# Per-partition scales for the two output weights, y's quarter sums with one operand from PSUM, and the order planned anew

## The chip, the cores and the metric

The kernel runs on 1 core of a Trainium2 chip. The metric is the device time of one execution in microseconds, the median of 3 runs. Engines: PE (matrix products), PEld (its weight loads), DVE (vector), ACT (activation), POOL (general), SP (transfers).

## The reference, cut to what matters

```python
scores = scale * q @ k.transpose(0, 1, 3, 2)          # 4 batches, 8 heads, 576 x 64
scores = where(scores >= max(scores) - tau, scores, -1e9)
x = softmax(scores) @ v                               # to 2304 tokens x 512
h = x @ w_in                                          # 512 x 2048
x = (h * tanh(log1p(exp(min(h, 20))))) @ w_out        # layer 1; h itself over 20
h = x @ w2_in
out = (h * clip(h + 3, 0, 6) / 6) @ w2_out            # layer 2
```

The four weights arrive as 64-bit floats; everything else is 32-bit.

## The kernel before, in words

**Number format.** A product of 32-bit numbers is made as three products of 16-bit halves: each operand is scaled by a power of two and split into a high and a low half (`hi` on ACT, `lo`, a subtraction, on POOL or DVE). The scales need maxima.

**Weights.** The matrices are numbered m = 0 (w_in), 1 (w_out), 2 (w2_in) and 3 (w2_out), and come in 8 groups each of 128 partitions x 1024 pairs of words (`raw_lr`). `maximum` (L442, DVE) finds the largest value of each partition. `group_scale` makes a scale from it: a cut to the exponent (`cut`, L453), then `spread`, then `factor` (L456 to L460). `spread` gives every partition the maximum over all 128: `diag` puts the column on a diagonal matrix (tasks `zd`, tile `dgb_zd`, on ACT L413 or DVE L415), `total` multiplies it by ones on PE (`zp`, L418) and `top` takes the row maximum on DVE (`zt`, L421). Steps `c1` to `c4` then join the two words of each number. `summary` combines the eight groups' scales of a matrix. For m = 2 and 3, `combined` makes sums of quarters of the weights (tiles `sum_h`, `sum_q`).

**Stages.** Attention runs from 0 to about 430 us with the first matmul of layer 1 (`h_g`, L834) laid between its score tiles (`s_s`, L1448) and products with v (`aux_pv`, L1496); the exponentials pass to the latter through transposing DMAs (`pt_tr`). Layer 1's second matmul (`y_y`, L948) runs from 486 to 702 in 9 blocks of 256 tokens, 192 matmuls each, with two y tiles in PSUM. Weights of m = 1, 2 and 3 are converted under both. Layer 2 runs from 713: 7 products of quarters instead of 8 for each unit (`h_g0a`, `hp_g1a` and so on, L1021, 24 matmuls each; then L1168), whose operands are sums of quarters.

**y to layer 2.** `split_sums` takes the maximum of a block of y (L664), spreads it (`zpy`, the same PE step), copies the scaled block from PSUM to `xf` on ACT (`take`, L728), forms four quarter sums (`four_sums`, L703 and L383) and splits them (`yl_zhy`). The same `four_sums` makes the sums of the activated values (`g_ab`) in layer 2, on POOL.

**Order.** Every task goes to a planner (`Plan`) while the program is built. It holds a cost for each task and engine, due times and the constants at the head of the file, picks the engine where several may do a task (`WHO`), and so fixes the sequence of every engine. On the chip each engine runs its sequence in that order and stops at an instruction that is not ready. For the kinds of DVE tasks listed in `PORT` the planner reckons with no start ahead of the end of POOL's last task, which holds for the sums of `g_ab` and of the weights (`q`), and not for those of y:

```python
if e == "dve" and task.kind in PORT:
    t = max(t, self.clock["pool"])
```

Of the kernel before, what the change touches and what calls it, by code (L numbers as in the profile page):

```python
# [16 lines left out]
ALU = mybir.AluOpType  # L17
# [19 lines left out]
Q = BLK // 2  # L37
# [3 lines left out]
ORDER_OUT = (0, 5, 6, 4, 2, 3, 1)  # L41
INF_BITS = 0x7F800000
TINY = 2.0 ** -100
WARM_WINDOW = 3.413
RELEASE = dict.fromkeys(("s", "m", "h", "y", "aux"), 0.27)

STEP = 2.55
START = 7.2
PV_OFF = 3.72
V_FIRST = 1.0  # L50
DIRECT_AHEAD = 8.0
DIRECT = 1
PREP_AHEAD = 2.45
CONV_STEP = 2.06
CONV_AT = 3.0
LATE_STEP = 1.5
OUT_STEP = 2.39
OUT_AT = 0.0
V_AHEAD = 6.29
MOE_OFF = 9.75  # L60
MOE_LAG = 15.8
RATE = 1.32
NX = 3
FLIP = 1.61
ALPHA = {"act": 3.07, "pe": 6.71}
FITS = 0.09
# [19 lines left out]
SLACK = 0.26
SLOW = 0.75
SLOW_LATE = 0.162
HASTE = -9.076
WHO = {  # L90
    "c20": ("pool", "dve"), "c21": ("pool",), "c30": ("dve",), "c31": ("pool", "dve"),
    "q2": ("dve",), "q3": ("pool", "dve"), "u20": ("pool", "dve"), "u21": ("pool",),
    "u30": ("pool",), "u31": ("pool", "dve"), "qy": ("dve",), "uy0": ("pool", "dve"), "uy1": ("pool", "dve"),
    "q": ("pool",), "o0": ("dve",), "o1": ("pool",),
}
NBLK_EARLY = 2 * B - 1
EASE = {"mk": -1.41, "ph": -0.76, "pl": -3.92, "tr": -1.06, "ex": 0.6, "s": -3.68, "th": -3.16}
P_LO = ("pool",)
EXPAND = {"act": 1.15}
BUFS = {"e": 3, "p16": 3}  # L100
LATE = {"gs": 2, "hl": 2, "h": 2, "y": 2}
WINDOW = {"pe": 0.26, "dve": 0.05, "act": 0.02, "pool": 0.15, "sp": 0.21}
NEAR_LATE = {"pe": 0.577, "dve": 0.049, "act": 0, "pool": 0.004, "sp": 0.21}
OFF_LATE = 0
OFF_FINAL = 22.457
LATE_AT = 2.5
OFF_SECOND = 27.972
# [71 lines left out]
class Plan:  # L179
# [157 lines left out]
def fused_kernel(ctx: ExitStack, tc, q, k, v, tau, w1i, w1o, w2i, w2o, out):  # L337
    nc = tc.nc
# [46 lines left out]
    def pick(which, **cost):  # L385
        return {e: cost[e] for e in WHO[which]}
# [5 lines left out]
    NG = NF // 2  # L392
# [11 lines left out]
    def bits(t):  # L404
        return t.bitcast(U32)
# [60 lines left out]
    def summary(task, m, after):  # L466

        w = wsc[m]  # L470
# [20 lines left out]
        return task({"dve": 1.6}, scales, after, [], f"zs{m}")  # L491
# [13 lines left out]
    def convert(m, src, pool, prio, off, ring):  # L505
        if m not in wsc:
            scale_columns(m)
        if m < 2:
            r_w[m] = Ring(f"w{m}_", maker(pool, f"w{m}_", [P, 2, 2, DM], F16), NG)
            wt[m] = [Buf(r_w[m]) for _ in range(NG)]  # L510
            for w in wt[m]:
                w.left += 1
        elif m == 2:
            r_w[m] = Ring(f"w{m}_", maker(pool, f"w{m}_", [P, 7, 2 * P], F16), 2 * NG)
        if m > 1:
            wt[m] = [(Buf(r_w[m]), Buf(r_w[m])) for _ in range(NG)]
# [72 lines left out]
    def combined(m, g, t, after, task):  # L589
# [103 lines left out]
    def four_sums(task, name, tile_of, bufs, after, width, who):  # L693


        def at(k):
            return tile_of()[:, :, k]

        def differ(e):
            sub(e, at(6), at(0), at(1))  # L700

        def add_right(e, dst, k):
            engine[e].tensor_tensor(at(dst), at(k), at(2), ALU.add)  # L703

# [12 lines left out]
    def split_sums(task, name, src, dst, inverse, ring, deps):
# [255 lines left out]
    def second_layer(blk):  # L973
# [117 lines left out]
        def finish(g, part, first, done):  # L1091
# [745 lines left out]
```

## Time and profile before

| | |
|---|---|
| median of 3 runs | 1054.19 us (1052.78 to 1055.12) |
| profiled execution | 1054.73 us; its span 1052.9 us, so 1.8 us lie around the span |
| busy, share of the span | PE 969.1 us (92%), DVE 782.6 (74%), ACT 667.7 (63%), POOL 638.1 (61%) |
| mean granted clock of PE | 0.965 of full speed |

The rows below are from that execution. A wait names the engine that released it last; the clock is the share of 2.4 GHz that was granted.

### The profile page before, as it was taken

How to read it: one execution, taken by the hardware profiler on the slowest of the kernel's cores; microseconds unless marked ns; L12 is line 12 of the kernel's file. 1: busy time of each engine (PE TensorE's matmuls, PEld its weight loads, DVE VectorE, ACT ScalarE, POOL GpSimd, SP SyncE). 2: the span in 40 equal slices, each digit the busy share in tenths (PEclk: the TensorE clock that was granted, in tenths of full speed). 3: DMA queues.
4: the chain of work that ended last, by engine and by line, in shares of the span. 5: the costliest groups of instructions: out<-in, count | busy, mean ns of one | idle time of the engine just before them, and what ended most of it. 6: DMA issues, size and time to landing. Idle time of an engine off the chain costs nothing.

```text
span 1052.9 us, 26050 instructions
## 1 busy us (share of the span) xinstructions
PE 969.1 (92%) x10790; PEld 857.7 (81%) x10790; DVE 782.6 (74%) x1385; ACT 667.7 (63%) x1048; POOL 638.1 (61%) x544
## 2 busy tenths in 40 slices
PE   4789799999899988999998999989999999999997
PEld 2566478888888877888887888779999999999985
DVE  5887788788878778758999999996464645545563
ACT  5666668799788887657777877736444444444441
POOL 1676856566565667634554677745757566564664
PEclk9997669999999999999999999989999999999998
DMA  9865959999999999985475656564011101101001
GB/s 267 181 167 132 223 119 220 222 247 240 202 233 211 197 221 214 249 296 222 161 255 195 215 198 241 212 239 150 2 57 56 28 31 57 57 1 57 22 16 27
DMA packets 199336, 166.85 MB, mean 158 GB/s; under 512 B 174129, under 2 KB 174641, under 8 KB 192817
## 3 DMA queue, kind: packets, MB, share of 16 engines
q1 hardware_dynamic: 199216, 165.18, 59.0%
q8 instruction: 85, 1.39, 0.5%
q14 instruction: 35, 0.28, 0.1%
HBM read 86.64 MB, written 36.04 MB: 117 GB/s over the span
## 4 chain that ended last, share of the span: by engine, by line
PE 50%; DVE 25%; DMA 13%; ACT 5%; issue 4%; POOL 3%; SPq 1%; DVEq 0%; ACTq 0%; POOLq 0%
DMA pt_tr<-p_ph 8%; PE s_s L1448 6%; PE h_g L834 6%; PE h_g0a L1021 5%; PE hp_g1a L1021 4%; PE aux_pv L1496 3%; DVE gs_h L928 3%; DVE e_ex L1470 3%; PE y_y L948 2%; PE h_g0d L1021 2%; PE hp_g1d L1021 2%; DVE nm_pk L1457 2%; POOL p_ph L383 2%; DMA v_lv<-in_v 2%; DMA raw_lr<-in_moe_w_out 1%
## 5 line engine op out<-in xcount | busy, mean ns | idle before, releaser
L383 POOL TENSOR_TENSOR p_ph<-e_ex,p_ph 128x128 f16<-128x128 f32 (+3 forms) x160 | 190.9, 1215 | 108.2 <-ACT p_ph L1475 79.1
L1168 PEld LDWEIGHTS <-gs_h 128*128 128x128 f16 x1512 | 147.2, 98 | 19.2 <-issue 2.2
L1021 PEld LDWEIGHTS <-w__h 128*128 128x128 f16 x2016 | 157.9, 99 | 5.5 <-issue 4.7
L1457 DVE TENSOR_REDUCE nm_pk<-s_s 128x1 f32<-128x576 f32 x144 | 105.9, 751 | 36.2 <-PE s_s L1448 35.6
L1470 DVE SCALAR_TENSOR_TENSOR e_ex<-s_s,thr_th,e_ex 128x576 f32<-128x576 f32 x144 | 112.2, 811 | 18.1 <-ACT thr_th L1462 12.4
L703 POOL TENSOR_TENSOR g_ab<-g_ab 128x256 f32<-128x256 f32 x72 | 60.3, 848 | 106.2 <-DVE g_ab L1108 104.9
L1467 ACT ACTIVATE e_ex<-s_s,nm_pk 128x576 f32<-128x576 f32 x144 | 104.1, 732 | 24.7 <-DVE nm_pk L1457 17.8
L1496 PEld LDWEIGHTS <-pt_tr 128*128 128x128 f16 x2016 | 84.2, 105 | 30.5 <-DMA pt_tr<-p_ph 24.2
L1496 PE MATMUL aux_pv<-vh,pt_tr 128*128 128x65 f16 (+1 forms) x1296 | 91.1, 207 | 18.4 <-DMA pt_tr<-p_ph 18.0
L1475 ACT ACTIVATE p_ph<-e_ex 128x576 f16<-128x576 f32 x144 | 94.9, 680 | 18.5 <-DVE e_ex L1470 13.2
L383 DVE TENSOR_TENSOR gs_h<-g_ab,gs_h 128x896 f16<-128x896 f32 x36 | 52.3, 1456 | 68.8 <-ACT gs_h L1118 68.8
L1021 PEld LDWEIGHTS <-w__u 128*128 128x128 f16 x1008 | 99.3, 99 | 0.0
L1118 ACT ACTIVATE gs_h<-g_ab 128x1792 f16<-128x1792 f32 x36 | 59.2, 1689 | 61.2 <-POOL g_ab L383 61.2
L383 POOL TENSOR_TENSOR gs_h<-g_ab,gs_h 128x896 f16<-128x896 f32 x36 | 85.2, 2385 | 8.8 <-ACT gs_h L1118 8.8
L1108 DVE SCALAR_TENSOR_TENSOR g_ab<-g_ab,f 128x512 f32<-128x512 f32 x72 | 59.9, 878 | 9.9 <-ACT g_ab L1102 9.9
L1102 ACT ACTIVATE g_ab<-g_ab,aux,hscales 128x512 f32<-128x512 f32 x72 | 53.1, 803 | 16.9 <-DVE g_ab L1049 16.9
L383 POOL TENSOR_TENSOR g_ab<-g_ab 128x256 f32<-128x256 f32 x72 | 59.1, 832 | 1.3
L882 ACT ACTIVATE he_t<-h_g,hin 128x512 f32<-128x512 f32 x68 | 46.5, 684 | 18.2 <-PE h_g L834 14.6
L928 DVE SCALAR_TENSOR_TENSOR gs_h<-hp_e,fscales,gs_h 128x512 f16<-128x512 f32 x72 | 52.2, 739 | 2.2 <-ACT gs_h L922 1.9
L919 ACT ACTIVATE hp_e<-hl_l 128x512 f32<-128x512 f32 x72 | 42.2, 594 | 15.6 <-DVE gs_h L928 15.4
L1448 PE MATMUL s_s<-kda_kh,qsa_qp 128*128 128x288 f32 x160 | 49.2, 326 | 1.7 <-DVE den_dt L1571 0.7
L1448 PE MATMUL s_s<-kda_lk,qsa_qp 64*128 64x288 f32 x80 | 35.6, 604 | 15.3 <-DVE e_ex L1470 8.2
(690 smaller groups left out, 2955.3 us busy)
## 6 DMA issues: line engine op xcount, KB each, us to landing
hd<-he_t SPq DMA_DIRECT2D x36, 512.0 KB, 3.5
hl_l<-hd SPq DMA_DIRECT2D x18, 1024.0 KB, 6.1
raw_lr<-in_moe_w_in SPq DMA_DIRECT2D x16, 1024.0 KB, 5.6
raw_lr<-in_moe_w_out SPq DMA_DIRECT2D x16, 1024.0 KB, 6.3
yd<-yl_zhy SPq DMA_DIRECT2D x9, 896.0 KB, 5.0
rk_lk<-in_k SPq DMA_DIRECT2D x12, 576.0 KB, 4.7
rq_lq<-in_q SPq DMA_DIRECT2D x12, 576.0 KB, 5.6
v_lv<-in_v SPq DMA_DIRECT2D x16, 320.0 KB, 4.7
```

The lines of the kernel that those rows point to most:

```text
L383: engine[e].tensor_tensor(dst, a, b, ALU.subtract)
L703: engine[e].tensor_tensor(at(dst), at(k), at(2), ALU.add)
L834: mm(hv[:, j, :], wj[:, wl, c * P : (c + 1) * P], x.tile[:, c, xl, :], start=j == 0 and n == 0, stop=j == 1 and n == 11, skip_group_check= ...
L928: nc.vector.scalar_tensor_tensor(s.tile[:, k, 1], g.tile.rearrange("p (a n) -> p a n", a=2), fs[:, fp : fp + 1], s.tile[:, k, 0], ALU.mult ...
L1021: mm(dst.tile[:, i * Q : (i + 1) * Q], wt[2][fp][wl].tile[:, right - 1, c * P : (c + 1) * P], x[xl].tile[:, c, left - 1], start=first and ...
L1168: mm(region(p), part[:, gl, left - 1], wt[3][fp][wl].tile[:, right - 1], start=fp == n == 0 and spot(p)[1] == 0, stop=fp == NG - 1 and n == 2,
L1448: mm(s[j].tile[:, half, :HALF], lh, rh[:, half * HALF : (half + 1) * HALF], start=m == 0, stop=m == len(terms) - 1,)
L1457: nc.vector.tensor_reduce(neg.tile[:, j : j + 1], sv(j), AX.XY, ALU.max, negate=True)
L1467: nc.scalar.activation(ev(j), sv(j), AF.Exp, bias=neg.tile[:, j : j + 1])
L1470: nc.vector.scalar_tensor_tensor(ev(j), sv(j), thr.tile[:, j : j + 1], ev(j), ALU.is_ge, ALU.mult)
L1475: nc.scalar.activation(p16.tile[:, js, :S], e_.tile[:, js], AF.Copy)
L1496: mm(ov[:, dst, :d], pt.tile[:, j, ch, :], part.tile[:, src, vc, :], start=i == j == ch == 0 and part is vh, stop=j == w - 1 and ch == 8, ...
```

## The change

It has three parts. First, for m = 1 and 3 the cut and the spread of each group go: each partition has a scale of its own, from its own maximum (with a floor of 2^-13), and `summary` takes the maximum over the groups in each partition and spreads that once (`zps`), after which a new task `rows` makes the factors. That removes 16 tasks each of `za`, `zp` and `zt`, with their diagonals, and adds 2 `zps`. Second, the four sums of a block of y become scalar_tensor_tensor instructions on DVE that scale and combine one operand straight from PSUM and one from SBUF, one behind the other; y's tile is held until the last of them. Third, the planner's constants are all set anew, and a table `PAD` lets it reckon `zp`, `zpy` and `zps` as ready on PE 1.3 to 3 later than their operand. By the new order POOL gives 144 sums of layer 2 (128x256) to DVE, and takes 24 weight sums (`sum_h`, `sum_q`; 8 of 128x512 and 16 of 128x256) from DVE.

```diff
-STEP = 2.55
-START = 7.2
-PV_OFF = 3.72
+STEP = 2.554
+START = 9.737
+PV_OFF = 2
...
-    "q": ("pool",), "o0": ("dve",), "o1": ("pool",),
+    "q": ("dve",), "o0": ("dve",), "o1": ("pool", "dve"),
...
+PAD = {"zp": 1.326, "zpy": 3, "zps": 3}
...
+            if e == "pe":
+                t += PAD.get(task.kind, 0.0)
...
         def factor(e):
-            nc.vector.tensor_scalar(top, top, TINY, None, ALU.max)
+            nc.vector.tensor_scalar(top, top, FLOOR, None, ALU.max)
...
-        a = task({"dve": 0.15}, cut, [after], [], "za" + name)
-        a = spread(task, name, lambda: top, [], ring, a)
+        a = after
+        if m % 2 == 0:
+            a = task({"dve": 0.15}, cut, [a], [], "za" + name)
+            a = spread(task, name, lambda: top, [], ring, a)
...
+        if m % 2 == 0:
+            return task({"dve": 2.4}, scales, after, [], f"zs{m}")
+        a = task({"dve": 0.9}, scales, after, [], f"zs{m}")
+        a = spread(task, f"s{m}", lambda: w["c"][:, 0:1], [], ring, a)
+        return task({"dve": 0.4}, rows, [a], [], f"zr{m}")
...
-        made = four_sums(task, name, lambda: xf.tile, [xf], [a], 2 * Q, "qy")
+
+        def quarter(j, t):
+            return src.tile[:, j].rearrange("p (c t n) -> p c t n", c=2, t=2)[:, :, t]
+
+        def combine(dst, part, other, op):
+            nc.vector.scalar_tensor_tensor(dst, part, s0(), other, ALU.mult, op)
...
+        for n, fn in enumerate((differ, add_right(5, 6), last, add_right(4, 0))):
+            a = task({"dve": 0.4}, fn, [a], [src, xf, sm], f"v{name}_{n}")
+        made = [a]
```

**How the order moves.** On DVE, in layer 1's second matmul, this is the last group of w2_out (m = 3, group 7) of before: `top_6824` and `sc_6825` are its maximum and scale, `gs_h` the operand of the y matmuls.

```order
L442 TENSOR_REDUCE top_6824<-raw_lr_7_0_9734 128x1
L928 SCALAR_TENSOR_TENSOR gs_h_0_8_1_9838<-hp_e_0_8_1_9786,fscales,gs_h_0_8_1_9838 128x512
L559 SCALAR_TENSOR_TENSOR cvt_c_6__1_9696<-raw_lr_6_0_9532,cvt_c_6__1_9696 128x1024
L453 TENSOR_SCALAR top_6824<-top_6824 128x1
L928 SCALAR_TENSOR_TENSOR gs_h_0_8_1_9838<-hp_e_0_8_1_9820,fscales,gs_h_0_8_1_9838 128x512
L664 TENSOR_REDUCE sm_zmy_7_0_7_1_9889<-y_y_0_0_7_0_9580 128x1
L421 TENSOR_REDUCE top_6824<-h_zp_7_1_9895 128x1
L667 TENSOR_SCALAR sm_zmy_7_0_7_1_9889<-sm_zmy_7_0_7_1_9889 128x1
L456 TENSOR_SCALAR top_6824<-top_6824 128x1
L457 TENSOR_SCALAR sc_6825<-top_6824 128x1
L460 TENSOR_SCALAR sc_6825<-sc_6825 128x1
```

The same group in the changed kernel:

```order
L446 TENSOR_REDUCE top_6786<-raw_lr_7_0_9718 128x1
L460 TENSOR_SCALAR top_6786<-top_6786 128x1
L461 TENSOR_SCALAR sc_6787<-top_6786 128x1
L464 TENSOR_SCALAR sc_6787<-sc_6787 128x1
L479 TENSOR_SCALAR s_6788<-sc_6787 128x8
L480 TENSOR_SCALAR s_6788<-s_6788 128x8
L481 TENSOR_SCALAR is_6789<-s_6788 128x8
L482 TENSOR_SCALAR is_6789<-is_6789 128x8
L484 TENSOR_REDUCE c_6793<-is_6789 128x1
```

The cut and the row maximum over PE's `h_zp` are gone, and the scale follows the group's maximum at once, then the summary's first steps up to the maximum over the groups (`c_6793`).

On PE, at the head of layer 2, this is where the spread of the last block of y (`zpy_8`) stands in before:

```order
L1021 LDWEIGHTS w__u_3_0_3_8000
L1021 MATMUL hp_g0b_0_0_10227<-xl_x__1_0_0_9788,w__u_3_0_3_8000 128x128
L418 LDWEIGHTS ones
L418 MATMUL h_zpy_8_0_8_1_10258<-dgb_zdy_8_0_8_1_10256,ones 128x128
L1021 LDWEIGHTS w__h_0_0_2_7565
L1021 MATMUL h_g0a_0_0_10198<-xl_x__1_0_0_9788,w__h_0_0_2_7565 128x128
```

And in the changed kernel:

```order
L1052 LDWEIGHTS w__u_3_0_3_7958
L1052 MATMUL h_g0d_0_0_10199<-xl_x__1_0_0_9660,w__u_3_0_3_7958 128x128
L422 LDWEIGHTS ones
L422 MATMUL h_zpy_8_0_8_1_10335<-dgb_zdy_8_0_8_1_10164,ones 128x128
L1052 LDWEIGHTS w__h_4_0_2_8079
L1052 MATMUL h_g1b_0_0_10345<-xl_x__1_0_0_9660,w__h_4_0_2_8079 128x128
```

Ahead of it stand 2 products of layer 2 (48 matmuls) in before and 8 (192 matmuls) now, counted from block 8's last `y_y`. For the other blocks `zpy` comes 24 to 60 `y_y` and `h_g` matmuls behind its block's last in before, and 60 to 96 now; the fewest then left before the block after next begins to fill the same y tile are 96. `zps_3` stands 96 `y_y` matmuls ahead of the end of block 8.

On POOL, this is the first unit of block 8 in layer 2, near the program's end, in before:

```order
L703 TENSOR_TENSOR g_ab_1_8_2_14935<-g_ab_1_8_2_14935 128x2x128
L383 TENSOR_TENSOR g_ab_1_8_2_14935<-g_ab_1_8_2_14935 128x2x128
L703 TENSOR_TENSOR g_ab_1_8_2_14935<-g_ab_1_8_2_14935 128x2x128
L703 TENSOR_TENSOR g_ab_1_8_3_14936<-g_ab_1_8_3_14936 128x2x128
L383 TENSOR_TENSOR g_ab_1_8_3_14936<-g_ab_1_8_3_14936 128x2x128
L383 TENSOR_TENSOR g_ab_1_8_2_14935<-g_ab_1_8_2_14935 128x2x128
```

In the changed kernel these stand on DVE, behind the last step of the activation (L1139):

```order
L1139 SCALAR_TENSOR_TENSOR g_ab_1_8_2_14853<-g_ab_1_8_2_14853,f_6783 128x512 x2
L1139 SCALAR_TENSOR_TENSOR g_ab_1_8_3_14854<-g_ab_1_8_3_14854,f_6783 128x512
L716 TENSOR_TENSOR g_ab_1_8_2_14853<-g_ab_1_8_2_14853 128x2x128
L387 TENSOR_TENSOR g_ab_1_8_2_14853<-g_ab_1_8_2_14853 128x2x128
L1139 SCALAR_TENSOR_TENSOR g_ab_1_8_3_14854<-g_ab_1_8_3_14854,f_6783 128x512
L716 TENSOR_TENSOR g_ab_1_8_2_14853<-g_ab_1_8_2_14853 128x2x128
L716 TENSOR_TENSOR g_ab_1_8_3_14854<-g_ab_1_8_3_14854 128x2x128
```

The sums change engine; the subtractions `gs_h` behind them stay divided between DVE and POOL.

## Rows read from the trace of the kernel before

**Rows 1.** Windows by stage: stretch, its us, busy us (count) of each engine, clock, DMA
```profile
73.00:95.00 22.00, 19.95 (x126) 13.65 (x126) 16.98 (x31) 13.14 (x21) 15.67 (x16) 0.53 0.64 143
...
111.00:149.00 38.00, 32.55 (x169) 23.00 (x170) 30.81 (x56) 24.94 (x40) 28.14 (x24) 0.51 0.70 166
149.00:430.00 281.00, 260.27 (x3206) 232.37 (x3204) 230.45 (x404) 231.36 (x426) 178.93 (x158) 0.99 1.02 220
...
702.00:713.00 11.00, 6.46 (x79) 6.33 (x77) 8.01 (x23) 2.08 (x4) 2.02 (x1) 0.69 0.52 193
713.00:1014.00 301.00, 301.00 (x4151) 286.29 (x4149) 168.07 (x275) 137.96 (x176) 186.77 (x167) 1.00 0.13 44
```

**Rows 2.** Windows, the two halves of layer 1's second matmul
```profile
486.00:600.00 114.00, 107.67 (x987) 95.68 (x985) 107.32 (x192) 86.64 (x132) 64.24 (x41) 1.00 0.62 219
600.00:702.00 102.00, 96.35 (x895) 85.43 (x893) 96.46 (x172) 74.16 (x108) 72.23 (x51) 1.00 0.63 224
```

**Rows 3.** Waits of PE, 430 to 702: us in total, times, longest
```profile
PE h_zp L418 <- ACT dgb_zd L413: 8.6, 9, 2.1
PE h_zpy L418 <- ACT dgb_zdy L413: 2.3, 3, 1.7
PE h_zp L418 <- DVE dgb_zd L415: 2.0, 2, 1.7
```

**Rows 4.** Waits of PE, 430 to 486
```profile
PE h_zp L418 <- ACT dgb_zd L413: 1.5, 3, 0.6
```

**Rows 5.** Waits of PE, 600 to 702
```profile
PE h_zp L418 <- ACT dgb_zd L413: 2.8, 3, 1.2
```

**Rows 6.** Chain that ended last, 484 to 494: start us, us, what
```profile
485.72 7.86 PE y_y L948 x72
```

**Rows 7.** Waits of PE, 702 to 713
```profile
PE h_zpy L418 <- DVE dgb_zdy L415: 4.5, 1, 4.5
```

**Rows 8.** Timeline of DVE, 700 to 708
```profile
704.80 1.07 DVE L383 TENSOR_TENSOR yl_zhy<-xf_zvy,yl_zhy 128x896 f16<-128x896 f32 x1
705.80 1.21 DVE L664 TENSOR_REDUCE sm_zmy<-y_y 128x1 f32<-128x1024 f32 x1
```

**Rows 9.** Chain that ended last, 700 to 716
```profile
707.84 2.56 PE h_g0a L1021 x24
710.40 2.18 PE h_g0d L1021 x24
712.58 1.34 PE h_g0a L1021 x24
```

**Rows 10.** Waits of PE, 1014 to 1053
```profile
PE y_y__1_8_0_15461 L1168 <- DVE out_va L1212: 2.0, 1, 2.0
```

**Rows 11.** Timeline of DVE, 1010 to 1026
```profile
1016.95 4.71 DVE L383 TENSOR_TENSOR gs_h<-g_ab,gs_h 128x896 f16<-128x896 f32 x2
```

**Rows 12.** Waits of PE, 0 to 430
```profile
PE aux_pv L1496 <- DMA pt_tr<-p_ph: 17.8, 17, 3.7
...
PE aux_zp L418 <- ACT dgb_zd L413: 2.3, 2, 2.2
```

**Rows 13.** Groups by line on DVE, whole span: busy us, mean ns, idle time before
```profile
L703 DVE TENSOR_TENSOR xf_zvy<-xf_zvy 128x256 f32<-128x256 f32 x18 | 14.0, 780 | 3.9 <-ACT xf_zvy L728 3.8
...
L383 DVE TENSOR_TENSOR xf_zvy<-xf_zvy 128x256 f32<-128x256 f32 x18 | 12.9, 718 | 0.0
```

**Rows 14.** Line 1212 on DVE: duration ns min/median/max, first and last start
```profile
L1212 DVE SCALAR_TENSOR_TENSOR out_va<-y_y___1_1_0_11350,xscale,out_v x2: 473/473/473, 799.3 to 800.9; 128x256 f32<-128x256 f32 x2
```

**Rows 15.** Timeline of DVE, 572 to 577
```profile
574.03 1.62 DVE L703 TENSOR_TENSOR xf_zvy<-xf_zvy 128x256 f32<-128x256 f32 x1
```

**Rows 16.** Timeline of POOL, 572 to 577
```profile
573.73 1.64 POOL L383 TENSOR_TENSOR w__u<-cvt_c__1_8329,w__h 128x768 f16<-128x768 f32 x1 [2.09 <-ACT w__h L614]
```

**Rows 17.** Groups by line and form on POOL, 707 to 1010
```profile
L383 POOL TENSOR_TENSOR gs_h<-g_ab,gs_h 128x896 f16<-128x896 f32 x32 | 75.1, 2366 | 8.2 <-ACT gs_h L1118 8.2
L703 POOL TENSOR_TENSOR g_ab<-g_ab 128x256 f32<-128x256 f32 x65 | 54.9, 854 | 100.3 <-DVE g_ab L1108 99.2
```

More of the change, by code (lines that the diff above doesn't have):

```diff
@@ L43 @@
 TINY = 2.0 ** -100
+FLOOR = 2.0 ** -13
 WARM_WINDOW = 3.413
 RELEASE = dict.fromkeys(("s", "m", "h", "y", "aux"), 0.27)
-STEP = 2.55
-START = 7.2
-PV_OFF = 3.72
-V_FIRST = 1.0
-DIRECT_AHEAD = 8.0
-DIRECT = 1
[L53 to L59, printed above, removed]
+STEP = 2.554
+START = 9.737
+PV_OFF = 2
+V_FIRST = -0.697
+DIRECT_AHEAD = 6.547
+DIRECT = 1
+PREP_AHEAD = 6
+CONV_STEP = 1
+CONV_AT = 2.543
+LATE_STEP = 6.434
+OUT_STEP = 2.112
+OUT_AT = 14.379
+V_AHEAD = 3
 MOE_OFF = 9.75
-MOE_LAG = 15.8
-RATE = 1.32
+MOE_LAG = 12.613
+RATE = 1.061
 NX = 3
-FLIP = 1.61
-ALPHA = {"act": 3.07, "pe": 6.71}
-FITS = 0.09
+FLIP = 3.654
+ALPHA = {"act": 2.28, "pe": 3.707}
+FITS = 0.193
 PORT = ("kl", "vl", "c", "ql", "u", "o", "zs", "q", "p")
@@ L85 @@
 PV_DEEP = 2
[L86 to L89, printed above, removed]
+SLACK = 0.067
+SLOW = 1.002
+SLOW_LATE = 0.352
+HASTE = -0.174
 WHO = {
-    "c20": ("pool", "dve"), "c21": ("pool",), "c30": ("dve",), "c31": ("pool", "dve"),
-    "q2": ("dve",), "q3": ("pool", "dve"), "u20": ("pool", "dve"), "u21": ("pool",),
-    "u30": ("pool",), "u31": ("pool", "dve"), "qy": ("dve",), "uy0": ("pool", "dve"), "uy1": ("pool", "dve"),
-    "q": ("pool",), "o0": ("dve",), "o1": ("pool",),
+    "c20": ("dve",), "c21": ("pool", "dve"), "c30": ("pool", "dve"), "c31": ("pool", "dve"),
+    "q2": ("pool", "dve"), "q3": ("pool", "dve"), "u20": ("pool",), "u21": ("pool",),
+    "u30": ("pool", "dve"), "u31": ("pool",), "uy0": ("pool", "dve"), "uy1": ("pool", "dve"),
+    "q": ("dve",), "o0": ("dve",), "o1": ("pool", "dve"),
 }
 NBLK_EARLY = 2 * B - 1
-EASE = {"mk": -1.41, "ph": -0.76, "pl": -3.92, "tr": -1.06, "ex": 0.6, "s": -3.68, "th": -3.16}
+EASE = {"mk": -2.863, "ph": 0.251, "pl": -2.376, "tr": -5.713, "ex": -1.859, "s": -3.718, "th": -5.465}
 P_LO = ("pool",)
@@ L101 @@
 LATE = {"gs": 2, "hl": 2, "h": 2, "y": 2}
[L102 to L107, printed above, removed]
+WINDOW = {"pe": 0.251, "dve": 0.108, "act": 0.02, "pool": 0.211, "sp": 0.203}
+PAD = {"zp": 1.326, "zpy": 3, "zps": 3}
+NEAR_LATE = {"pe": 0.189, "dve": 0.174, "act": 0.102, "pool": 0.849, "sp": 0.21}
+OFF_LATE = 1.876
+OFF_FINAL = 21.161
+LATE_AT = 16.754
+OFF_SECOND = 30.466
 class Ring:
@@ L460, in factor, with summary @@
             nc.vector.tensor_scalar_mul(sc, sc, 2.0 ** -112)
-        a = task({"dve": 0.15}, cut, [after], [], "za" + name)
-        a = spread(task, name, lambda: top, [], ring, a)
+        a = after
+        if m % 2 == 0:
+            a = task({"dve": 0.15}, cut, [a], [], "za" + name)
+            a = spread(task, name, lambda: top, [], ring, a)
         return task({"dve": 0.45}, factor, [a], [], "zf" + name)
-    def summary(task, m, after):
+    def summary(task, m, ring, after):
         w = wsc[m]
@@ L489, in scales, with rows @@
             ts(w["f"], w["is"], w["c"][:, 1:2], None, ALU.mult)
-        return task({"dve": 1.6}, scales, after, [], f"zs{m}")
+        def rows(e):
+            ts = nc.vector.tensor_scalar
+            ts(bits(w["c"][:, 1:2]), bits(w["c"][:, 0:1]), INF_BITS, None, ALU.bitwise_xor)
+            ts(w["f"], w["is"], w["c"][:, 1:2], 0.5, ALU.mult, ALU.mult)
+        if m % 2 == 0:
[3 more added lines that the diff above has]
+        return task({"dve": 0.4}, rows, [a], [], f"zr{m}")
     def tasker(at):
@@ L526, in convert @@
             one_conversion(m, g, raw, [loaded, factors[g]], task)
-        scaled_by[m] = summary(tasker(prio + 2 * NG * off), m, factors)
+        scaled_by[m] = summary(tasker(prio + 2 * NG * off), m, ring, factors)
     def one_conversion(m, g, raw, deps, task):
@@ L570, in one_conversion @@
         ]
-        a = task({"dve": 1.22}, c3, b, [raw, t], "c" + nm)
-        a = task({"dve": 1.22}, c4, [a], [raw, t], "c" + nm)
+        a = task({"dve": 1.28}, c3, b, [raw, t], "c" + nm)
+        a = task({"dve": 1.28}, c4, [a], [raw, t], "c" + nm)
         if m > 1:
@@ L622, in combined @@
             a = task(
-                pick(f"q{m}", pool=0.1 + 0.59 * size, dve=0.1 + 0.27 * size), fn, [a], [t, sums],
+                pick(f"q{m}", pool=0.1 + 0.65 * size, dve=0.15 + 0.3 * size), fn, [a], [t, sums],
                 f"q{nm}{n}",
@@ L708, in go @@
         def go(fn, deps, n):
-            cost = pick(who, pool=0.1 + width / 450, dve=0.1 + width / 960)
+            cost = pick(who, pool=0.74, dve=0.4)
             return task(cost, fn, deps, bufs, f"q{name}_{n}")
@@ L739, in split_sums, with differ, add_right, last @@
         a = task({"act": 1.37}, take, [a], [src, xf, sm], "zv" + name)
-        made = four_sums(task, name, lambda: xf.tile, [xf], [a], 2 * Q, "qy")
+        def quarter(j, t):
+            return src.tile[:, j].rearrange("p (c t n) -> p c t n", c=2, t=2)[:, :, t]
+        def combine(dst, part, other, op):
+            nc.vector.scalar_tensor_tensor(dst, part, s0(), other, ALU.mult, op)
+        def differ(e):
+            combine(xf.tile[:, :, 6], quarter(0, 0), xf.tile[:, :, 1], ALU.subtract)
+        def add_right(dst, k):
+            return lambda e: combine(xf.tile[:, :, dst], quarter(1, 0), xf.tile[:, :, k], ALU.add)
+        def last(e):
+            combine(xf.tile[:, :, 7], quarter(1, 1), xf.tile[:, :, 5], ALU.subtract)
+        for n, fn in enumerate((differ, add_right(5, 6), last, add_right(4, 0))):
+            a = task({"dve": 0.4}, fn, [a], [src, xf, sm], f"v{name}_{n}")
+        made = [a]
         a = task({"act": 1.7}, hi, made, [xf, dst], "zh" + name)
@@ L1126, in finish @@
                     go(
-                        pick(f"o{k}", pool=2.05, dve=1.05), lambda e, k=k: lo(e, k), [a], [g, part],
+                        pick(f"o{k}", pool=2.35, dve=1.2), lambda e, k=k: lo(e, k), [a], [g, part],
                         f"o{first}_{k}",
```

4 lines of the change are left out of this document (1 added, 3 removed).

## The prediction

> **What bounds the kernel now.** I read the windows by stage first. In layer 2, 713 to 1014, PE is busy 301.00 of 301 us at full clock [rows 1]: nothing there can get faster unless matmuls go, and the change takes none away. In layer 1's second matmul PE is busy 107.67 + 96.35 = 204.0 of 216 us, and DVE almost as long, 107.32 + 96.46 = 203.8 [rows 2]. The two are coupled: PE's idle 12 us should be read as waits, so the waits of PE come next. They are nearly all waits of `zp` and `zpy`, the spreading matmuls, for their diagonal: 8.6 + 2.0 us for `zp` and 2.3 for `zpy` [rows 3]. The wait itself is short work; it is long because PE reaches the matmul before the maximum behind which the diagonal stands has had its turn on DVE.
>
> The turn from layer 1 to layer 2 is the third view. PE waits 4.5 us for the diagonal of block 8's y [rows 7]. What is late is DVE: its maximum over y starts at 705.80, behind the split of the block before [rows 8]. After that wait the granted clock of the stretch is 0.69, between the levels of 1.2 and 2.4 GHz [rows 1], and the chain shows two products at 2.56 and 2.18 us where the next takes 1.34 [rows 9].
>
> In attention, 149 to 430, PE is busy 260.27 of 281 us; ahead of that lie two stretches of 22 and 38 us with a granted clock of 0.53 and 0.51 [rows 1]. PE's waits there are led by the products with v for their transposed exponentials, 17.8 us in 17 waits [rows 12].
>
> **Part 1, scales per partition.** A group of w_in's kind keeps its spread, a group of m = 1 or 3 loses it. By time, the `zp` waits divide into m = 1 before 486, m = 2 in the first half of the second matmul, m = 3 after 600. For m = 3 it is 2.8 us on ACT's diagonals [rows 5] and 2.0 on DVE's, all of it in this half [rows 3]: 4.8 us, which go with the instructions that waited. For m = 1 it is 1.5 [rows 4]; two `zps` come, and I count 0.5 back, so 1.0. Below, the two new spreads cost nothing if PE comes late to them; above, 3 us each, near the longest such wait (2.1) and the chain behind it. `zps_1` stands 60 matmuls before the first `y_y`, which needs the factors: 60 x 7.86/72 [rows 6] = 6.5 us, and behind it lie a row maximum, three small DVE instructions and one scaling each on ACT and DVE, my estimate 3 us. `zps_3` has 96 matmuls, 10.5 us. So no wait there.
>
> The removed matmuls are 14 of 128x128, some 0.1 us each: 1 to 2 us, left out of the sum as part of the noise.
>
> **Part 2, sums from PSUM.** Before, a block's four sums take 14.0 + 12.9 us over 36 instructions, 0.75 each [rows 13]. The nearest row for the new form, one PSUM and one SBUF operand at the same size on DVE, is the output's, 473 ns in all of its cases [rows 14]. So 36 x 0.473 = 17.0, and DVE gives back 9.9 us, off the path unless DVE is late, for which see part 3. Why the old form varies shows at 574: a sum takes 1.62 us [rows 15] and ends with a POOL instruction that runs 1.64 us [rows 16].
>
> The Trainium skill (SBUF — State Buffer, Who interferes with whom) says that a DVE instruction with at most one SBUF input doesn't contend with GpSimd, and that one with two does, the loser blocking for the other's whole instruction. By that rule the saving is between nothing and 1.2 us an instruction, 0 to 41 us of DVE time over 36; the mean in the rows puts it at 9.9. The pair at 574 agrees with the rule.
>
> The price is that y is held longer. Block 6 is the tightest: 96 matmuls, 10.5 us, from its spread to block 8's first matmul. DVE does the row maximum, three small ones, two scalings of the operand, two conversion steps and the four sums in between, some 0.3 + 0.5 + 1.5 + 2.5 + 1.9 = 6.7 us by an estimate from like instructions. That fits by 4 us. If DVE comes later than that, every us is a us of PE.
>
> **Part 3, the new order.** `PAD` moves the spreads back in PE's sequence. For `zpy` the distance grows from 24 to 60 matmuls (2.6 to 6.5 us) to 60 to 96 (6.5 to 10.5 us). All 2.3 us of waits should go; I take 2.0. For the `zp` of m = 2 the waits are 8.6 - 1.5 - 2.8 = 4.3 us; a padding of over 1 us, where the longest wait is 2.1, should leave 1.5, so 2.8. The bounds here are 0 and 4.3.
>
> At the turn, 8 products stand before `zpy_8` instead of 2, so 6 x 1.34 = 8 us [rows 9] more room for a wait of 4.5: I take 4.0. The clock should then not fall: 2.56 + 2.18 - 2 x 1.34 = 2.1 us.
>
> DVE gives 24 weight sums to POOL. At POOL's 0.854 us for 128x256 [rows 17] the 8 double and 16 single ones are 32 x 0.854 = 27 us there. POOL is busy 64.24 + 72.23 = 136.5 us in the second matmul [rows 2], so it has room, with 164 of 205. DVE, at 203.8, falls by the sums' 9.9, by 32 x 0.47 to 0.75 [rows 13, 14] = 15 to 24 for the weight sums, and by a few for the maxima, to about 172: it no longer runs level with PE. This is what makes me believe that the waits go rather than move.
>
> In layer 2, DVE takes over 144 sums, of which 128 or so fall between 713 and 1014. At 0.75 [rows 13] they add 96 to its 168.07 us: 264 of 301. PE stays the bound and the edit costs nothing there; its cover is 37 us. At the tail PE waits 2.0 us for DVE [rows 10], which is held in two subtractions of 4.71 us together [rows 11] while POOL runs its sums. The sums leave POOL, but DVE gets them: from -2.0, the whole wait, to +4.0, 8 sums at 0.75 [rows 13] less those 2.0, and I take -1.3, nearer the first, since the sums that ran on POOL beside the two subtractions are gone.
>
> In attention the sequence differs everywhere, and the trace can't tell what the new one does. One wait surely changes: `zp` of the first group, 2.3 us [rows 12], now stands two score tiles further back. The distance from a tile's scores to its product with v, counted in matmuls of the order and priced by their durations, is on the mean of the last 60 tiles 13.4 us now against 12.9, but its least is 7.1 against 10.3. I take 3 us, with bounds of -16 and +31 from the rivals below.
>
> **Sum.** 4.8 + 1.0 + 2.8 + 2.0 + 4.0 + 2.1 + 1.3 + 3 = 21.0 us. From the profiled 1054.7 that is 1033.7. The profiled execution lies 0.5 us above the median, so 1033 us.
>
> **Rivals.**
> - A, attention gains more. A stretch at half clock [rows 1] goes with its cause, a late transpose. PE's 32.55 us of work in 111 to 149 would take some 16 less at full clock, the 19.95 in 73 to 95 some 10 less. For it: the mean distance to the product with v grows. Against: both stretches lie early, where the number of score tiles ahead is small in both orders. Time 1017 to 1023.
> - B, slower: transposes late at attention's end. Tiles 73 to 76 of 80 have 11.5, 8.9, 7.1 and 8.0 us from scores to product now, against 15.5, 11.8, 10.8 and 10.3. If the chain of maximum, exponential, split and transpose takes over 10 us there, some five tiles wait 3 us each, 15 us, and PE's clock may halve for another 38 us, as it did before at 111: 16 us. That is +31 on 1033, about 1064, slower than before; it decides at 21 us. With the waits alone it is 1048. For it: 17 such waits, up to 3.7 us, are there before [rows 12]. Against: they fall early mostly.
> - C, layer 2 bound by DVE. Its two-operand sums meet POOL's subtractions of 2.366 us [rows 17]. A block takes 301/8.1 = 37.1 us; DVE would need 264/8.1 = 32.6. Two blocked subtractions a block fill the rest; a third makes 39.7 - 37.1 = 2.6 us a block, +21 in all, so about 1054. For it: the sum at 574. Against: the mean of 0.75 has such cases in it already. The Trainium skill (Perfetto Trace Analysis, Optimizing Scalar/DVE Operations) warns that offloading between GpSimd and DVE might not help because they share a port.
> - D, the waits of the second matmul move instead of going: DVE remains late, and y's tile or the remaining `zp` waits for it. Then half of the 10.6 us of the `zp` and `zpy` terms is lost, and up to 4 us at block 8: about 1043.
>
> **Chances.** The forecast 0.60, with its own range of 1025 to 1042; A 0.14; B 0.13, half of it over 1054; C 0.07; D 0.06. Faster by over 0.2%, about 2 us, which is what a measurement of this kernel can tell from none: 0.60 + 0.14 + 0.06 + half of B and a third of C, 0.89. Within 2 us: 0.03. Slower: 0.08. The range runs from A's lower end to the milder case of B: 1017 to 1049.
>
> **What the profile after should show.** No `zp` wait after 600 and less than 2 us before it; `zpy` waits under 0.5 us; DVE busy some 170 of a stretch of about 205 us in the second matmul; y's sums at 473 ns without spread; no fall of the clock at the turn, and no wait of 4.5 us; layer 2 as before, 37.1 us a block with PE always busy and DVE below 265. The prediction is wrong if PE waits for `gs_h` or for y's tile in the second matmul, if PE has gaps in layer 2, or if the waits of `aux_pv` in attention are far from 17.8 us: above 25 is B, below 8, or a clock near 1 from 73 to 149, is A.

## The result and the profile after

The changed kernel takes 1039.86 us, the median of 4 runs (1039.42 to 1040.66), against 1053.49 of before in the same comparison: the ratio is 0.9872, with an interval of 0.9853 to 0.9891, so it is 13.6 us faster by the medians. The forecast was 1033. The profiled execution took 1039.59 us with a span of 1037.4, PE busy 92% of it, DVE 75%, ACT 65% and POOL 53%.

The span is best cut at two instructions: the first `y_y` matmul, with which layer 1's second matmul begins, and the first `h_g0a`, with which layer 2 begins. Each time below is the first start of that instruction in the trace of that kernel, and the stage is their difference.

| profiled execution | first `y_y` | first `h_g0a` | span | second matmul | from layer 2 on |
|---|---|---|---|---|---|
| before | 485.6 | 700.2 | 1052.9 | 214.6 | 352.7 |
| changed | 481.2 | 683.9 | 1037.4 | 202.7 | 353.5 |

So between these two executions, whose spans differ by 15.5 us, the gain is 4.4 us up to the second matmul and 11.9 in it, and 0.8 is lost behind it. These are the windows of the changed kernel around the turn: stretch, its us, busy us (count) of PE, PEld, DVE, ACT and POOL, clock, DMA.

```profile
481.00:684.00 203.00, 203.00 (x1870) 182.11 (x1868) 176.32 (x314) 152.89 (x229) 148.94 (x104) 1.00 0.64 226
684.00:698.00 14.00, 10.61 (x156) 10.27 (x154) 12.13 (x30) 4.94 (x7) 6.28 (x5) 0.88 0.29 112
698.00:713.00 15.00, 14.09 (x251) 13.85 (x249) 12.04 (x28) 10.09 (x16) 2.41 (x1) 1.00 0.62 224
713.00:998.00 285.00, 282.28 (x3832) 267.29 (x3830) 184.72 (x365) 136.71 (x179) 83.56 (x32) 1.00 0.12 38
```

In the second matmul PE has no idle time left (before, 204.0 of 216 [rows 2]), and DVE is busy 176 of 203 us where it was level with PE. Both are what the forecast said. At the turn the forecast did not hold: PE is busy 10.61 of 14 us, and even behind it 2.7 us are missing, in a stage where before had none [rows 1]. The waits of PE in the changed kernel from 684 to 713 (us in total, times, longest) name another instruction than before, where it was `zpy` [rows 7]:

```profile
PE h_g0a L1052 <- ACT s_ka L1070: 3.1, 2, 2.2
PE h_g0a L1052 <- DMA xl_x__1_1_0_10377<-yd: 0.5, 1, 0.5
PE h_g1b L1052 <- DVE sm_zmy L425: 0.4, 1, 0.4
PE h_g0a L1052 <- DMA xl_x__1_0_0_10037<-yd: 0.3, 1, 0.3
```

The chain that ended last shows two slow products here too, as in [rows 9]:

```profile
693.11 2.42 PE h_g0a L1052 x24
695.53 2.04 PE hp_g1a L1052 x24
697.58 1.34 PE h_g0a L1052 x24
```

`s_ka` is the copy on ACT that frees the PSUM buffer of a product. The timeline of ACT in the changed kernel shows what stands ahead of the second one:

```profile
692.17 0.40 ACT L417 ACTIVATE dgb_zdy<-ident,sm_zmy 128x128 bf16<-128x128 f32 x1 [4.17 <-DVE sm_zmy L680]
692.48 0.58 ACT L1070 ACTIVATE s_ka<-h_g0a 128x512 f32<-128x512 f32 x1
```

ACT stood idle for 4.17 us at the diagonal of y's last block, which waits for DVE. The timeline of DVE says why that is late:

```profile
686.66 1.63 DVE L1017 TENSOR_SCALAR hscales<-b,xscale 128x8 f32<-128x8 f32 x1
...
688.50 1.88 DVE L1017 TENSOR_SCALAR hscales<-b,xscale 128x8 f32<-128x8 f32 x1
...
690.73 1.22 DVE L677 TENSOR_REDUCE sm_zmy<-y_y 128x1 f32<-128x1024 f32 x1
```

The maximum over block 8 comes 7 us after y's last matmul, behind the scales (`hscales`) of six blocks; those of the later five layer 2 needs 37 us and more later. With `zpy` moved back 6 products, the wait went to the next instruction on ACT that stood behind the same lateness.

Most of these 7 us are not work. The same scale of 128x8 takes 0.23 us at 690.59, but 1.63 and 1.88 at 686.66 and 688.50, and these two end at 688.29 and 690.38, within 0.03 us of an instruction of POOL:

```profile
686.38 1.89 POOL L387 TENSOR_TENSOR yl_zhy<-xf_zvy,yl_zhy 128x896 f16<-128x896 f32 x1
688.22 2.13 POOL L387 TENSOR_TENSOR st_u<-sum_h,st_h 128x1024 f16<-128x1024 f32 x1
```

The six scales ahead of the maximum take 5.8 us, where six at 0.23 would take 1.4: DVE was held for 4.4 us beside POOL. The same is in before, which the prediction didn't see: the last scale ahead of the late maximum there [rows 8] starts at 701.84, takes 2.20 us and ends 0.03 us after an instruction of POOL.

### The profile page after: what moved, and what is told of

It reads as the page before. It is cut to its first block, busy times and chain, and to the rows that moved or that the text cites. A ratio compares the mean times of both kernels' runs of the same rounds, so it can differ in the third digit from the quotient of the medians.

```text
span 1037.4 us, 25967 instructions
## 1 busy us (share of the span) xinstructions
PE 959.5 (92%) x10776; PEld 853.8 (82%) x10776; DVE 776.5 (75%) x1454; ACT 672.2 (65%) x1058; POOL 548.5 (53%) x421
## 4 chain that ended last, share of the span: by engine, by line
PE 65%; DMA 12%; DVE 10%; ACT 4%; issue 4%; POOL 3%; SPq 0%; DVEq 0%; POOLq 0%; ACTq 0%
PE y_y L979 16%; DMA pt_tr<-p_ph 10%; PE h_g L865 10%; PE s_s L1479 7%; PE h_g0a L1052 4%; PE hp_g1a L1052 4%; PE aux_pv L1527 3%; POOL p_ph L387 2%; PE hp_g1d L1052 2%; PE h_g0d L1052 2%; DVE e_ex L1501 1%; PE h_g1b L1052 1%; ACT e_ex L1498 1%; PE y_y__1_8_0_15376 L1199 1%; PE y_y___1_1_0_11177 L1199 1%
## 5 line engine op out<-in xcount | busy, mean ns | idle before, releaser
L387 POOL TENSOR_TENSOR p_ph<-e_ex,p_ph 128x128 f16<-128x128 f32 (+3 forms) x160 | 187.1, 1191 | 103.2 <-ACT p_ph L1506 84.6
L387 POOL TENSOR_TENSOR gs_h<-g_ab,gs_h 128x896 f16<-128x896 f32 x36 | 94.5, 2639 | 219.4 <-ACT gs_h L1149 219.1
L387 DVE TENSOR_TENSOR gs_h<-g_ab,gs_h 128x896 f16<-128x896 f32 x36 | 48.5, 1350 | 17.7 <-ACT gs_h L1149 17.7
L1080 DVE TENSOR_TENSOR g_ab<-h_g0d,s_ka 128x256 f32<-128x256 f32 x36 | 13.6, 419 | 58.9 <-PE h_g0d L1052 41.2
L1139 DVE SCALAR_TENSOR_TENSOR g_ab<-g_ab,f 128x512 f32<-128x512 f32 x72 | 52.5, 767 | 2.5 <-ACT g_ab L1133 2.5
L953 ACT ACTIVATE gs_h<-hp_e,fscales 128x512 f16<-128x512 f32 x72 | 46.2, 679 | 7.2 <-PE y_y L979 5.1
L446 DVE TENSOR_REDUCE top<-raw_lr 128x1 f32<-128x1024 f32 x32 | 38.9, 1215 | 10.1 <-DMA raw_lr<-in_moe_w_out 5.5
```

The lines of the kernel that those rows point to most:

```text
L387: engine[e].tensor_tensor(dst, a, b, ALU.subtract)
```

## The experiments

Ten of the twelve runs hold the order fixed: the sequence of tasks and the engine of each, as the planner chose them for before or for the changed kernel, is written into the kernel as a list and followed. So a part can be changed without anything else being planned anew. Where stages are compared below, they are those of the runs' profiled executions, cut as in the table above. The common edit in `Plan.run`:

```diff
-            _, e, (start, task) = best
+            name, e = ORDER_GIVEN[self.at]
+            self.at += 1
+            task = next((t for t in self.open.get(e, ()) if t.name == name), None)
```

**The scales alone** (before's order; the tasks `za`, `zd`, `zp`, `zt` of m = 1 and 3 taken from the list, two `zps` put in).

```diff
-        a = task({"dve": 0.15}, cut, [after], [], "za" + name)
-        a = spread(task, name, lambda: top, [], ring, a)
+        a = after
+        if m % 2 == 0:
...
```

> The order of before, held fixed, with the scales per partition alone (the spreads of w_out's and w2_out's groups left out, two spreads of their summaries put in). Theory: PE's zp waits of these two matrices, 4.8 + 1.0 us, were time on the path, so 5 to 7 us faster than before (1047 to 1049), and no zp wait after 600. Rival (the gain of the whole change comes from the new order and not from this): within 2 us of before, the waits turning up at other instructions of the second matmul.

Measured: 1055.11 us, ratio 1.0018 (0.9998 to 1.0037). No gain; the theory falls. The 12 runs spread from 1047.69 to 1059.25, and the profiled one is the longest of them, so its total is not read, only its second matmul and the waits there. The stage takes 215.2 us, as in before (214.6). Its window:

```profile
488.80:704.00 215.20, 203.31 (x1843) 180.19 (x1841) 200.88 (x337) 159.11 (x233) 135.70 (x89) 0.99 0.62 221
```

PE's waits in it, 488 to 704:

```profile
PE h_zpy L418 <- ACT dgb_zdy L413: 5.9, 6, 1.7
PE h_zp L418 <- ACT dgb_zd L413: 4.7, 3, 2.5
PE y_y L957 <- DVE gs_h L937: 1.3, 1, 1.3
```

The waits of w2_out's `zp` are gone, but `zpy` has 5.9 us instead of 2.3 [rows 3] and the kept `zp` 4.7. Together these are 11.9 us, where before has 12.0 from 486 to 702. Removing the instruction that waited moved the wait. The part also took 2.9 us of DVE's time (200.88 against 203.8), and these too gave nothing.

**The sums from PSUM alone** (before's order; the four tasks of each block keep their places).

```diff
-        made = four_sums(task, name, lambda: xf.tile, [xf], [a], 2 * Q, "qy")
+        for n, fn in enumerate((differ, add_right(5, 6), last, add_right(4, 0))):
+            a = task({"dve": 0.4}, fn, [a], [src, xf, sm], f"v{name}_{n}")
+        made = [a]
```

> The order of before, held fixed, with y's four sums from PSUM alone. Theory: DVE saves 10 us that lie beside PE's work, so 0 to 2 us faster. Rival (DVE runs level with PE in the second matmul and each us of it counts): 5 to 10 us faster. Second rival (y is held too long): PE waits for y's tile at the start of each block, 1 us a block or more, 7 us slower.

Measured: 1042.45 us, ratio 0.9894 (0.9874 to 0.9914). The first rival holds, though the gain is a little above its 5 to 10 us: four fifths of the whole gain come from an edit that the prediction put off the path. The second rival doesn't: no wait for y's tile appears. The second matmul takes 206.6 us, 8.0 less, and PE's waits in it come to 5.1 us. The window of its stage has DVE at 194 where [rows 2] add up to 203.8:

```profile
484.00:691.00 207.00, 201.92 (x1858) 180.21 (x1856) 194.16 (x359) 159.33 (x239) 135.85 (x90) 1.00 0.65 232
```

**Old forms with the new constants, and new forms with the old constants** (both planned, not held).

> The two old forms with all the new constants, the padding and the new costs, planned by them. Theory: the padding alone takes away most of the zp and zpy waits and attention gains its 4 us, but 16 spreads more load DVE and PE: 8 to 11 us faster than before. Rival (the new forms make the gain): under 4 us faster.

> The two new forms with all the constants of before and no padding, planned by them. Theory: the 5.8 us of the removed zp waits, and little else: 4 to 8 us faster than before. Rival (the new order makes all the gain): within 2 us.

Measured: 1081.95 us, ratio 1.0273 (1.0251 to 1.0295), and 1067.58, ratio 1.0133 (1.0113 to 1.0154). Both are slower than either kernel, and no expectation held. Of the first one PE's longest waits from 496 on, of the second one those from 706 on, show where:

```profile
PE h_g0a L1024 <- DMA xl_x__1_0_0_10208<-yd: 14.7, 1, 14.7
PE y_y L951 <- DVE gs_h L931: 11.6, 7, 3.4
PE h_zpy L421 <- ACT dgb_zdy L416: 10.1, 1, 10.1
```

```profile
PE h_g0a L1049 <- DMA xl_x__1_0_0_10101<-yd: 8.7, 1, 8.7
```

In each of the two the planner makes another order than in either kernel, so they can't say what a part is worth, which is why the others hold the order.

**Both parts in before's order** (the two edits above together).

> The order of before, held fixed, with the per-partition scales and the sums from PSUM, no new constants. New theory (DVE sets the second matmul of layer 1 in before, and every us of DVE time taken from it counts until PE's 203 us are reached): the sums alone gave 11 us; with the cuts and maxima gone too, 0 to 4 us more, about the changed kernel's time (1038 to 1043), so that the new order gives at most 3 us. Rival (the new order gives its own part): 1043 to 1050.

Measured: 1043.9 us, ratio 0.9908 (0.9878 to 0.9938), the same as the sums alone within the intervals, and just inside the rival's range. The new order's own part is therefore about 0.9908 - 0.9872, 4 us, but the two intervals overlap, and the median stands between two groups: three of the six times are 1041.4 to 1041.7 and three 1046.1 to 1046.8, for a reason that the record doesn't show. In the profile, one of the first three, the second matmul begins at 483.9 us against 481.2 in the changed kernel and takes 204.0 against 202.7, while layer 2 is 1.5 shorter. In the five profiles with before's order of attention the first `y_y` starts at 483.9 to 488.8, in the seven with the new order at 477.7 to 484.7, means of 485.3 and 481.0. Within each group the starts scatter by 2.1 us (standard deviation), so the difference of the means, 4.3 us with a standard error of 1.2, is clear of the scatter, while a single pair of profiles could not show it. Two of the first five, this run and the scales alone, already lack the spreads of m = 1 and start at 483.9 and 488.8, so nothing shows that these spreads have a part in it.

**The sums made twice**, in before's order and in the changed kernel's (the same values are written again; 36 more DVE instructions, 17 us).

```diff
             nc.vector.scalar_tensor_tensor(dst, part, s0(), other, ALU.mult, op)
+            nc.vector.scalar_tensor_tensor(dst, part, s0(), other, ALU.mult, op)
```

> The order of before, held fixed, with y's sums from PSUM, each of them made twice (36 more instructions of 0.476 us on DVE, 17 us, the same result). New theory (DVE's time counts one for one): 12 to 18 us slower than with the sums made once, so 1054 to 1060. Rival (what the new form gives is that it doesn't collide with POOL, and DVE's time as such is beside PE's): 0 to 5 us slower than with the sums made once, 1042 to 1047.

> The changed kernel's order, held fixed, with each of y's sums made twice (17 us more on DVE). New theory: DVE has 27 us of slack beside PE in the second matmul here, so 0 to 3 us slower than the changed kernel (1040 to 1043). Rival (DVE's time counts here too): 10 us or more.

Measured: 1059.24 us, ratio 1.0055 (1.0032 to 1.0079), 16.8 us over the sums made once; and 1045.81, ratio 0.993 (0.9902 to 0.9958), 6.0 over the changed kernel. In before's order the time of these sums on DVE counts one for one, with either sign. In the profile 12.8 of it lie in the second matmul (219.4 us) and 2.6 behind it. It is shown for the sums alone: the 2.9 us that the scales took from DVE gave nothing, so what a microsecond of DVE is worth depends on where in its sequence it lies. PE's waits in the second matmul of that run:

```profile
PE h_zp L418 <- ACT dgb_zd L413: 9.5, 8, 2.1
PE h_zp L418 <- DVE dgb_zd L415: 3.2, 2, 2.2
PE h_zpy L418 <- ACT dgb_zdy L413: 2.3, 3, 1.7
```

They come to 15.0 us, where with the sums made once they are 5.1. Not one of them is for y's tile, so it is not y's longer hold of its tile that counts but DVE's lateness, at whatever spread comes next. In the new order 27 us of slack take most of the 17; the expected 0 to 3 us were too few. In the profile 3.3 us are lost in the second matmul and 3.0 behind it. In the second matmul two kinds of wait appear that the changed kernel hasn't, the first of them for y's tile:

```profile
PE y_y L980 <- DVE xf_zvy L759: 2.1, 2, 1.5
PE h_zps L422 <- ACT dgb_zds L417: 0.8, 1, 0.8
```

The first is the price of holding y's tile, which the prediction named and put at nothing, with 4 us to spare at the tightest block: it is there already when the sums take 1.9 us a block longer.

**The spreads earlier** (the changed kernel's order; 16 spreads up to three PE tasks ahead). In the list, for the first of them:

```diff
+zp2_0 pe
 ...
-zp2_0 pe
```

> The changed kernel's order, held fixed, with the spreading matmuls of w2_in's 8 groups and y's first 8 blocks each up to three PE tasks (12 matmuls each) earlier, but behind their diagonal. Theory: the padding was worth the 4.8 us of the zp and zpy terms, so PE waits at them again and it is 3 to 6 us slower than the changed kernel. Rival (what freed PE was DVE's smaller load, which makes the diagonals come in time): within 1.5 us.

Measured: 1040.61 us, ratio 0.9866 (0.984 to 0.9892). The rival holds. PE waits for nothing in the second matmul with the spreads at either place, and this is its window:

```profile
480.00:682.00 202.00, 202.00 (x1861) 181.19 (x1860) 180.07 (x311) 152.84 (x228) 146.67 (x103) 1.00 0.64 226
```

**Layer 2's sums back on POOL** (the changed kernel's order).

```diff
-    "q": ("dve",), "o0": ("dve",), "o1": ("pool", "dve"),
+    "q": ("pool",), "o0": ("dve",), "o1": ("pool", "dve"),
```

> The changed kernel's order, held fixed, with the 144 sums of layer 2 back on POOL. Theory: PE bounds layer 2 either way, so within 3 us of the changed kernel; the 2.7 us that PE waits at 728 and near 740 go or stay. Rival C of the prediction (DVE's two-operand sums meet POOL's subtractions and cost time all through layer 2): faster by 5 us or more with the sums on POOL. Its reverse (POOL's slower sums come late): slower by over 5.

Measured: 1044.27 us, ratio 0.9912 (0.9889 to 0.9934), 4.4 us slower than the changed kernel, between the theory's 3 and the reverse's 5. Rival C is ruled out, and the move helped. The 4.4 may be too little: in this profile layer 2 takes 361.7 us against 353.5, 8.2 more, while the second matmul begins 3.5 us earlier, which is scatter, since up to there the two orders are the same. Of PE's waits from 713 to 1005 the first, for POOL in the first block, is one that the changed kernel hasn't; the second takes 1.0 us there:

```profile
PE y_y___1_0_0_10653 L1199 <- POOL gs_h L387: 3.1, 1, 3.1
PE hp_g1d L1052 <- DVE g_ab L1080: 2.9, 1, 2.9
```

**The turn** (the changed kernel's order, three runs): two places on ACT alone; DVE's maximum alone; both, with the scales of later blocks put behind block 0's first unit. In the list of the last one (`zmy` is the maximum, `zx` and `zo` are the scales):

```diff
 y17_0_0_8 pe
+zmy0_8_0_8 dve
+zby0_8_0_8 dve
+zx_1_0 dve
...
-zx_1_1 dve
...
 p3_1_0 dve
+zx_1_1 dve
+zo_1_1 dve
...
```

> The changed kernel's order, held fixed, but for two places on ACT at the head of layer 2: the copy s_ka of the first product goes ahead of a conversion step, and the diagonal of y's last block goes behind the copy of the third product. Theory: the 3.1 us that PE waits for these copies at the turn come from what stands ahead of them on ACT, the diagonal above all, which waits for DVE's late maximum; with them go the 2 us that the lower clock costs: 3 to 5 us faster than the changed kernel (1035 to 1037). Rival (the wait moves to the spread of y's last block, whose diagonal is no earlier): within 1 us of the changed kernel.

> The changed kernel's order, held fixed, but for DVE at the head of layer 2: y's last maximum goes ahead of the eight blocks' scales. Theory: the maximum at 690.7 was late because of those scales, and the copy behind its diagonal on ACT with it; it comes 5 us sooner and PE's longest wait there, 2.2 us, goes: 2 to 4 us faster than the changed kernel. Rival (ACT's conversion step is what holds the copies): within 1 us.

> The changed kernel's order, held fixed, but for the head of layer 2: y's last maximum and block 0's scales first on DVE, the scales of the later blocks behind the first unit of block 0, and the two copies on ACT ahead of the conversion step and the diagonal. Theory: the waits of PE at the turn come from DVE's 9 us of scales for blocks not yet needed, which hold y's maximum, the split of block 7 and the first sum that frees the buffer of the copies; with them gone, 3 to 6 us faster than the changed kernel (1034 to 1037). Rival (the last conversion of w2_out and the transfers behind it set the turn): within 1.5 us of it.

Measured: 1040.84 us (ratio 0.9879, 0.9855 to 0.9904), 1039.88 (0.9872, 0.9843 to 0.99) and 1036.77 (0.9829, 0.98 to 0.9858). The first two changed nothing that can be measured; each left 3 us or more of waits for `s_ka`. With DVE's maximum early, 684 to 713:

```profile
PE h_g0a L1052 <- ACT s_ka L1070: 3.2, 2, 1.9
PE h_g0a L1052 <- DMA xl_x__1_1_0_10377<-yd: 2.4, 1, 2.4
```

A later copy on ACT waits 4.59 us for the first sum on DVE (`g_ab`), which still stood behind the scales:

```profile
694.60 0.60 ACT L1070 ACTIVATE s_ka<-h_g0a 128x512 f32<-128x512 f32 x1 [4.59 <-DVE g_ab L1080]
```

The scales were held beside POOL here too (up to 1.88 us). With them out of the way, where POOL stands idle beside them and each takes 0.23 us, there is no wait for `s_ka` up to 713, the clock is full, and transfers and the first `gs_h` come next:

```profile
PE h_g0a L1052 <- DMA xl_x__1_1_0_10356<-yd: 1.5, 1, 1.5
PE y_y___1_0_0_10653 L1199 <- ACT gs_h L1149: 1.4, 1, 1.4
```

```profile
684.00:713.00 29.00, 25.42 (x440) 24.68 (x438) 23.39 (x61) 16.27 (x24) 10.68 (x7) 1.00 0.58 211
```

This version is the fastest of all, 3.1 us under the changed kernel by the medians, at the low end of the 3 to 6 expected, and 17.2 under before in its comparison; its interval meets that of the changed kernel at the edge, so that the step from the one to the other is likely rather than certain. Its profile, the longest of its six times, has 351.9 us from layer 2 on against 353.5. No run moves the scales away from POOL's instructions and leaves them ahead of the first sum, so how the gain divides between their place and POOL's hold on them is open.

## Why the prediction was right or wrong

The forecast had the sign, and the time within its range, but 7 us too much gain, and it credited the gain to the wrong part: that the second matmul came near its term is luck, since waits whose removal was worth nothing stood in for DVE's time, which the sum had left out.

- **Second matmul, 9.6 us forecast, 11.9 measured.** The size held, the reason didn't. The step that failed is "4.8 us, which go with the instructions that waited", with the 1.0 of m = 1. Held in before's order, that part gave nothing (1.0018), and PE's waits stayed at 11.9 us. The waits were priced as PE's own, when they were the places at which DVE's lateness shows: DVE was busy 203.8 of 216 us [rows 2], and 9.6 us less of it gave 8.0 in the stage, so the rest was not slack. The prediction had this as a condition, in "This is what makes me believe that the waits go rather than move" and in rival D, whose waits that move are what the run with the scales alone shows; it came in no term of the sum.
- **"DVE gives back 9.9 us, off the path unless DVE is late."** DVE was late. The size was right: 0.48 us a sum (472 to 485 ns over all 36), DVE's busy time in the stage down by 9.6, the stage by 8.0. It should have stood in the sum as 8 (the stage) to 11 (the medians). What was saved is time for which the old sums were held beside POOL: 13 of the 15 that took over 0.8 us end 0.27 to 0.29 us behind the end of an instruction of POOL, while the shortest took 0.41, less than the new form.
- **The padding, 2.0 + 2.8 us.** Worth nothing that could be measured in the changed kernel: with the spreads moved forward again the time stays (0.9866). That DVE's 176 us give them room fits this, and the waits that fell from 12.0 to 5.1 us with the sums alone.
- **The turn, 4.0 + 2.1 us.** The second step that failed. The extra 6 products were there, but the wait moved to `s_ka` (3.1 us), and the products at 2.42 and 2.04 us came back. The prediction had named "What is late is DVE" and then gave room to PE instead; it put the lateness down to the split ahead of the maximum, and not to the scales, long beside POOL, in front of that. The run with the scales moved puts the worth of the place at 1.6 (its profile) to 3.1 us (the medians), about half of the term at most.
- **Attention, 3 us, and m = 1, 1.0.** 4.4 in the two profiles, 4.3 on the means over five and seven. The sign and the size of the two together held, the cause is open; for the 1.0 of m = 1 nothing speaks. Rivals A and B did not come: the waits for transposed exponentials are 20.5 us now against 17.8 [rows 12], between the bounds of 8 and 25, and half clock remains early. But a part of what A described did: from 111 to 149 the clock is 0.69 where it was 0.51 [rows 1], 0.64 to 0.73 in all seven profiles of the new order against 0.51 to 0.55 in the five of the old. What that is worth, beside waits that grew, no run shows.
- **Tail, 1.3 us.** The wait is 1.2 against 2.0 [rows 10], 0.8 gained; the waits of 1.7 and 1.0 us at 728 and near 740, in block 0 and 1 of layer 2, take more than that. "The edit costs nothing there" was wrong by these 2.7 us, and gaps of PE in layer 2 were one of the prediction's own signs of being wrong; but the sums on POOL would cost 4.4 more.
- **Rival C** did not come: the sums on DVE took 0.42 and 0.44 us each on the mean, not 0.75. All but one of the 136 between 690 and 1000 lie near 0.42; one took 2.11. POOL was busy 83.56 of 285 us beside them; why they met it so seldom no run shows. The groups by line and form of the changed kernel on DVE, 690 to 1000 (busy us, mean ns, idle before):

```profile
L387 DVE TENSOR_TENSOR g_ab<-g_ab 128x256 f32<-128x256 f32 x68 | 28.9, 443 | 0.3
L716 DVE TENSOR_TENSOR g_ab<-g_ab 128x256 f32<-128x256 f32 x68 | 27.4, 417 | 0.1
```

The rule of the Trainium skill that the prediction weighed (SBUF — State Buffer, Who interferes with whom) agrees with the sums' spread: 407 to 1856 ns with two SBUF operands before, 472 to 485 with one from PSUM. The prediction left out a condition that the section puts with it, that the instruction is outside the modes that use both of DVE's port pairs; the scales at the turn, whose one tensor operand lies in SBUF, took up to 1.88 us beside POOL. They also read a factor for each partition, and no run shows whether that or the mode exposes them; one tensor operand in SBUF was not enough to keep clear. The warning of the Trainium skill that offloading between the two engines might not help (Perfetto Trace Analysis, Optimizing Scalar/DVE Operations) is not borne out here, where the kernel with the sums on DVE is 4.4 us faster than with them on POOL.

## What to carry to other kernels

Where two engines are busy almost equally long in a stage, suspect the one whose results the other waits for, and cost an edit by the time that it takes from that engine; the instruction at which the other one waits may be only where the lateness shows. To tell the two apart, add a known time to the suspect with the order held fixed: 17 us more on DVE cost 16.8 in the one order and 6.0 in the other. A wait that stands behind a late engine is moved, not removed, by giving its own instruction more room; look first at what the late engine does ahead of it that nobody needs yet, and whether the instructions there take longer than the same ones elsewhere.

## What was not expected of the hardware

An add of 128x256 with two SBUF operands took 0.72 to 0.78 us on the mean on DVE with POOL busy in the second matmul of before [rows 13], and 0.42 to 0.44 in layer 2 of the changed kernel with POOL busy 83.56 of 285 us. A scale of 128x8, 0.23 us by itself, took up to 2.20 us in before and 1.88 in the changed kernel, and the long ones end within 0.03 us of an instruction of POOL. And executions of the new order begin the second matmul anywhere from 477.7 to 484.7 us, a spread of 7 us in what is the same sequence up to there but for one run (the spreads earlier, at 480.0).
